# Routed experts of an FFT mixer: the last 20 tiles in steps of 64 tokens, second products on halves of the array

## The chip, the cores and the metric

The program runs on one core of a Trainium2 chip. The metric is the device time of the whole program in microseconds, median of three runs, lower is better. The profile is that of one more execution on the same core.

## What is computed

The input is `x` (8 sequences of 2496 tokens with 256 channels). Each sequence goes through a Fourier mixer, and every token of the result through one of eight experts:

```python
X = rfft(x, axis=1)
Yr = Xr @ w_r - Xi @ w_i + b_r          # likewise Yi
Yr = sign(Yr) * maximum(abs(Yr) - 0.01, 0)
y = irfft(Yr + 1j * Yi)                 # 19968 tokens of 256 channels
...
e_idx = argmax(y @ w_gate, axis=1)      # one expert of 8 for each token
for e in range(8):
    h = maximum(y[e_idx == e] @ w1[e], 0)      # 256 -> 1024: the first product
    ye = h @ w2[e]                             # 1024 -> 256: the second product
    out[e_idx == e] = gate_w * eom * ye
```

The products of the experts are made in float16 with a correction: each operand is split into a high and a low half, and three of the four partial products are added up (high x high, high x low, low x high).

## The kernel before

The kernel transforms the eight sequences one after the other. The routing sorts the tokens by expert and fills tiles of 128 tokens, each of one expert; this is done twice, once for the first four sequences (64 tiles, worked on in pairs that share an expert) and once for the rest (99 tiles, worked on singly), 163 tiles in all (`T_ALL`). The tiles of the first group fill gaps of the transform of the later sequences; from some 600 us on, the tail of the program is nearly all experts' tiles.

For each tile: `gathers` fetches 128 rows of `y` by an indirect DMA from GpSimd; `tokens` scales and splits them (VectorE, ScalarE), and a transposing DMA turns them, so that the channels lie on the partitions (`eT`); `fetch` loads the expert's weights into one of three buffers (`wbuf`), first half for `up`, second half for `down`.

`up` makes the first product. It is called twice for a single tile (`half`), each call filling one PSUM bank with 4 groups of 128 of the 1024 hidden channels. The stationary operand of each matmul is a block of 128x128 weights, the moving one is the tile's 128 tokens; a group is 6 matmuls (2 halves of the channels x 3 partial products), so a tile has 48. ScalarE then takes the bank to float16 with a Relu (L1489), VectorE writes what is lost by this rounding (L1490); the two are the high and low half of `hh`.

`down` makes the second product: stationary are 128 hidden channels by 128 tokens of `hh`, moving are 128x256 weights, and 24 matmuls (8 groups x 3) add up in one bank of 128 tokens by 256 channels. ScalarE scales it (L1461), and GpSimd scatters the rows to the output by an indirect DMA (L1464).

The order of all this is made by a planner in the program (`Issue`), which simulates the engines with the costs that each step names (`yield "P", r, 1.34, f`) and issues instructions in the order in which its model serves them. Steps with the smallest due time (`r`) go first. The planner knows none of the instructions' shapes; it knows the costs alone. In the tail its order on TensorE is: `up` of two tiles (four calls), then `down` of these two, and so on; the last tile stands alone.

Every matmul of these functions is preceded on TensorE by a load of its stationary operand (LDWEIGHTS), which the profile lists as PEld.

## Time and profile before

| | |
|---|---|
| time, median of 3 runs | 1435.92 us (1435.58 to 1435.95) |
| profiled execution | 1436.6 us, span 1434.8 us, mean granted clock 0.992 |
| TensorE busy | 1399.4 us, 98% of the span |
| weight loads busy | 1273.4 us, 89% |
| VectorE, ScalarE, GpSimd busy | 978.2, 738.6 and 636.3 us |
| first products of single tiles (L1479, 128 columns) | 4752 matmuls, 219 ns each from start to modelled end |
| second products (L1445) | 3912 matmuls, 273 ns each |

A matmul's length in the profile runs from its start to a modelled end, and several are in flight at once. So the time that one takes of TensorE isn't its length but the distance between starts: (length of an unbroken run - length of one) / (count - 1). Rows of weight loads (PEld) lie beside the matmuls, and an idle time of zero means that the engine was never without work between instructions. The forty slices of the page show busy tenths of each engine over the span; PEclk is the clock that TensorE was granted.

### The profile page before, as it was taken

The numbers are of one execution on the slowest core, as the hardware profiler recorded it, in microseconds if no ns is written. First come the engines' busy times: TensorE is split into PE (matmuls) and PEld (weight loads), VectorE is DVE, ScalarE is ACT, GpSimd is POOL, SyncE is SP. The second block draws the span as 40 slices with busy tenths as digits, with TensorE's granted clock in tenths as the row PEclk, the third lists the DMA queues.
The fourth block names the chain that finished last, engine by engine and source line by source line (L and its number), as shares of the span: only waits on it lengthen the run. The fifth ranks groups of instructions, "written<-read, shape, count | busy, mean of one in ns | idle before, by whom it ended". The sixth has DMA issues, their size and how long they took to land.

```text
span 1434.8 us, 42626 instructions
## 1 busy us (share of the span) xinstructions
PE 1399.4 (98%) x16436; PEld 1273.4 (89%) x16436; DVE 978.2 (68%) x2796; ACT 738.6 (51%) x1413; POOL 636.3 (44%) x729
## 2 busy tenths in 40 slices
PE   4999999999999998999999999999999999999998
PEld 4998887898888887888888888999999999999998
DVE  4887767788999896788888765554545545455452
ACT  4777676778687764433343344333334334333342
POOL 2274556266477563345455443333333343333411
PEclk8999999999999999999999999999999999999999
DMA  7779899998988789935372374533364233642342
GB/s 199 176 172 221 204 213 215 230 233 209 224 205 211 172 234 204 245 99 134 100 160 75 98 169 105 108 73 83 72 161 106 76 82 96 167 133 75 79 113 83
DMA packets 285652, 215.66 MB, mean 150 GB/s; under 512 B 240918, under 2 KB 249240, under 8 KB 281097
## 3 DMA queue, kind: packets, MB, share of 16 engines
q1 hardware_dynamic: 268887, 168.87, 49.6%
q0 software_dynamic: 15872, 42.83, 12.1%
q8 instruction: 129, 2.11, 0.6%
q10 hardware_dynamic: 690, 1.24, 0.3%
q14 instruction: 74, 0.61, 0.2%
HBM read 337.45 MB, written 58.91 MB: 276 GB/s over the span
## 4 chain that ended last, share of the span: by engine, by line
PE 46%; issue 29%; POOL 14%; DVE 6%; DMA 2%; ACT 1%; POOLq 0%; SPq 0%; ACTq 0%; DVEq 0%
PE ps L755 11%; PE ps L1479 9%; PE ps L1445 8%; POOL out L1464 7%; POOL yg L1348 7%; PE ps L647 5%; PE ps L851 3%; PE ps L785 3%; PE ps L725 3%; DMA x<-in_x 1%; PE ps L896 1%; PE ps L690 1%; PE ps L749 1%; PE ps L1277 1%; DVE z L771 1%
## 5 line engine op out<-in xcount | busy, mean ns | idle before, releaser
L1479 PE MATMUL ps<-eT,wbuf 128*128 128x128 f16 (+1 forms) x6288 | 458.9, 232 | 0.4 <-DMA wbuf<-wd 0.4
L1445 PE MATMUL ps<-wbuf,hh 128*128 128x256 f16 x3912 | 453.2, 273 | 0.0
L1479 PEld LDWEIGHTS <-wbuf 128*128 128x128 f16 x6288 | 418.9, 98 | 19.9 <-DMA wbuf<-wd 0.6
L1445 PEld LDWEIGHTS <-hh 128*128 128x128 f16 x3912 | 378.8, 98 | 44.2 <-issue 0.2
L1490 DVE SCALAR_TENSOR_TENSOR hh<-ps,hh 128x512 f16<-128x512 f32 x326 | 224.8, 690 | 267.6 <-ACT hh L1489 267.4
L1489 ACT ACTIVATE hh<-ps 128x512 f16<-128x512 f32 x326 | 194.6, 597 | 287.7 <-PE ps L1479 282.2
L1464 POOL DMA_INDIRECT out<-o,sidx x163 | 163.4, 1003 | 281.5 <-ACT o L1461 258.1
L1348 POOL DMA_INDIRECT yg<-yd,gidx x163 | 161.5, 991 | 247.1 <-DVE yhl L1374 211.5
L755 PE MATMUL ps<-whl,xt 128*128 128x256 f16 x1920 | 223.1, 273 | 0.7 <-ACT xt L740 0.7
L755 PEld LDWEIGHTS <-xt 128*128 128x128 f16 x1920 | 187.7, 98 | 32.1 <-ACT xt L740 1.1
L1461 ACT ACTIVATE o<-ps,facs 128x256 f32<-128x256 f32 x163 | 77.2, 473 | 229.5 <-PE ps L1445 149.0
L1374 DVE SCALAR_TENSOR_TENSOR yhl<-yg,ys,yhl 128x256 f16<-128x256 f32 x163 | 81.4, 506 | 62.4 <-ACT yhl L1373 62.3
L647 PEld LDWEIGHTS ps<-f1t,x 117*128 117x128 f32 (+1 forms) x704 | 87.1, 201 | 18.1 <-issue 15.8
L647 PE MATMUL ps<-f1t,x 117*128 117x120 f32 (+1 forms) x704 | 90.5, 285 | 0.2 <-ACT ste L802 0.2
L1373 ACT ACTIVATE yhl<-yg,ys 128x256 f16<-128x256 f32 x163 | 81.6, 501 | 13.9 <-DVE ys L420 5.9
L775 POOL TENSOR_TENSOR zhl<-z,zhl 128x512 f16<-128x512 f32 x54 | 62.8, 1162 | 49.8 <-ACT zhl L773 47.4
L1052 POOL TENSOR_TENSOR wsp<-wr,wsp 128x512 f16<-128x512 f32 x62 | 74.3, 1198 | 5.2
L785 PE MATMUL ps<-gt,zhl 128*128 128x128 f16 x960 | 65.5, 220 | 6.5 <-ACT zhl L773 3.7
L851 PE MATMUL ps<-bdt,f4t 120*117 120x512 f16 x264 | 71.0, 384 | 0.1
L656 ACT ACTIVATE at<-ps,sx 128x480 f16<-128x480 f32 (+1 forms) x88 | 55.7, 649 | 28.9 <-PE ps L647 26.3
L785 PEld LDWEIGHTS <-zhl 128*128 128x128 f16 x960 | 58.5, 98 | 13.4 <-ACT zhl L773 4.5
L770 ACT ACTIVATE zhl<-ps,sc 128x512 f32<-128x512 f32 x80 | 54.8, 685 | 25.6 <-PE ps L755 22.1
(195 smaller groups left out, 1651.0 us busy)
## 6 DMA issues: line engine op xcount, KB each, us to landing
wbuf<-wd SPq DMA_DIRECT2D x262, 1024.0 KB
yd<-yt SPq DMA_DIRECT2D x120, 158.4 KB
x<-in_x SPq DMA_DIRECT2D x114, 156.0 KB
wr<-in_moe_w SPq DMA_DIRECT2D x32, 512.0 KB
wd<-wsp SPq DMA_DIRECT2D x64, 256.0 KB
yg<-yd,gidx POOLq DMA_INDIRECT x163, 7.5
eT<-yhl SPq DMA_TRANSPOSE x163
out<-o,sidx POOLq DMA_INDIRECT x163, 2.4
```

The costliest lines, as they stand in the source:

```text
L647: T.matmul(pv[:, dh, :, m * j:m * j + m], xs[:k, j0 + j, 128 * dh:128 * dh + 128], fw, start=True, stop=True)
L755: T.matmul(yp[:, 256 * j:256 * j + 256], xt_[:, v, 2 * dh + j, 64 - 64 * u:192 - 64 * u], whl[:, dh, vw, 256 * u:256 * u + 256], start=Fal ...
L785: T.matmul(bv[:, j], zhl[:, vz, c:c + 128], gt[:, 2 * p + j, v], start=(n == 0), stop=(n == 2))
L851: T.matmul(pt[:P3], w, src[:, :, :, vb_], start=(n == 0), stop=(n == 2))
L1348: yield "G", r + 5.6 * t - 30, 1.0, lambda: G.indirect_dma_start(out=yg, out_offset=None, in_=src, in_offset=bass.IndirectOffsetOnAxis(ap= ...
L1373: yield "A", r - 10, 0.5, lambda: A.activation(yhl[:, 0], yg[:, :256], AF.Copy, scale=s)
L1374: yield "D", r - 10, 0.48, lambda: V.scalar_tensor_tensor(yhl[:, 1], yg[:, :256], s, yhl[:, 0], ALU.mult, ALU.subtract)
L1445: T.matmul(st["pt", t][1][:, :256], hh[:, v, fc, 128 * n:128 * n + 128], w[:, fc // 2, vw, fc % 2], start=(fc == k == 0), stop=(fc == 7 an ...
L1464: yield "G", r - DN, 1.0, lambda: G.indirect_dma_start(out=outs[t % 8], out_offset=bass.IndirectOffsetOnAxis(ap=sidx[:, t:t + 1], axis=0), ...
L1479: T.matmul(pt[:, 128 * m * j:128 * m * (j + 1)], w[:, dh, g // 4, vw, 128 * (g % 4):128 * (g % 4) + 128], eT[:, :m, v, dh], start=(n == 0) ...
L1489: yield "A", r, 0.6, lambda: A.activation(hv[:, 0], pt, AF.Relu)
L1490: yield "D", r, 0.69, lambda: V.scalar_tensor_tensor(hv[:, 1], pt, 0.0, hv[:, 0], ALU.max, ALU.subtract)
```

## The change

In the last 20 tiles (`t >= T_ALL - 20`), `up` writes each group of 128 columns in two steps of 64 tokens: all six matmuls for tokens 0 to 63, then all six for tokens 64 to 127. The weight blocks are loaded for each step anew, so a tile has 96 matmuls of 64 moving columns and 96 loads of 128x128 instead of 48 and 48.

`down` splits the stationary operand: for each of the 24 pieces there is one matmul for tokens 0 to 63, which writes PSUM partitions 0 to 63, and one for tokens 64 to 127, which writes partitions 64 to 127, both with the same 256 moving columns. The program marks the first as using columns 0 to 63 of the array and the second as using columns 64 to 127 (divisions of 128 rows by 64 columns), in turns. A tile has 48 matmuls and 48 loads of 64 columns instead of 24 and 24. All other matmuls of the program use the full array.

The costs that the planner is told stay the same, and so the order of steps on all engines does; the numbers of instructions on ScalarE, VectorE, GpSimd and SyncE are unchanged. On TensorE there are 34410 instructions where there were 31530 (20 tiles x 72 more matmuls and as many loads).

```diff
+HALVES = 20
 ...
 def down(t, m, n, w, hh, ih, r):
+        c = 64 if t >= T_ALL - HALVES else 128
         ...
             for fc in range(8 // m * half, 8 // m * (half + 1)):
                 for k, (v, vw) in enumerate(((0, 0), (0, 1), (1, 0))):
-                    T.matmul(st["pt", t][1][:, :256], hh[:, v, fc, 128 * n:128 * n + 128], w[:, fc // 2, vw, fc % 2], start=(fc == k == 0), stop=(fc == 7 and k == 2))
+                    for q in range(0, 128, c):
+                        T.matmul(st["pt", t][1][q:q + c, :256], hh[:, v, fc, 128 * n + q:128 * n + q + c], w[:, fc // 2, vw, fc % 2], start=(fc == k == 0), stop=(fc == 7 and k == 2))
 ...
 def up(t, m, half, w, eT, ie, hh, r):
-        c = 4 // m
+        cn = 4 // m
+        c = 64 if t >= T_ALL - HALVES else 128 * m
         def f(i):
             pt = bank(i)
-            for j in range(c):
-                g = c * half + j
-                n = 0
-                for dh in range(2):
-                    for vw, v in ((0, 0), (0, 1), (1, 0)):
-                        T.matmul(pt[:, 128 * m * j:128 * m * (j + 1)], w[:, dh, g // 4, vw, 128 * (g % 4):128 * (g % 4) + 128], eT[:, :m, v, dh], start=(n == 0), stop=(n == 5))
-                        n += 1
+            for j in range(cn):
+                g = cn * half + j
+                for q in range(0, 128 * m, c):
+                    n = 0
+                    for dh in range(2):
+                        for vw, v in ((0, 0), (0, 1), (1, 0)):
+                            tok = eT[:, :, v, dh] if m > 1 else eT[:, 0, v, dh, q:q + c]
+                            T.matmul(pt[:, 128 * m * j + q:128 * m * j + q + c], w[:, dh, g // 4, vw, 128 * (g % 4):128 * (g % 4) + 128], tok, start=(n == 0), stop=(n == 5))
+                            n += 1
             return pt
```

(In `up` the name `c` for the number of groups becomes `cn` in the lines behind it too.)

Two places in TensorE's order are shown. In the rows the line stands first, then the instruction; a matmul's row names the PSUM bank, the moving operand or weights and the shape as output partitions or rows by moving columns (128x64: 64 columns; 64x256: 64 output partitions). L1479 is L1486 after the change, L1445 is L1449. First, where `up` of two tiles ends and `down` begins (the first time both are changed), before:

```order
L1479 MATMUL ps1_25857<-eT0_9665,wbuf0_9304 128x128
L1479 LDWEIGHTS wbuf0_9304
L1479 MATMUL ps1_25857<-eT0_9665,wbuf0_9304 128x128
L1445 LDWEIGHTS hh1_9931
L1445 MATMUL ps4_25886<-wbuf2_9430,hh1_9931 128x256
```

and after:

```order
L1486 MATMUL ps1_26001<-eT0_9665,wbuf0_9304 128x64
L1486 LDWEIGHTS wbuf0_9304
L1486 MATMUL ps1_26001<-eT0_9665,wbuf0_9304 128x64
L1449 LDWEIGHTS hh1_9931
L1449 MATMUL ps4_26054<-wbuf2_9430,hh1_9931 64x256
```

Nothing moved past anything: the same steps follow each other, with the loads and matmuls of each made smaller and twice as many, and the division of the array changes with the line.

Second, where `down` of the two tiles ends and `up` of the next begins, before:

```order
L1445 MATMUL ps7_25688<-wbuf1_9305,hh0_9904 128x256
L1479 LDWEIGHTS wbuf2_9430
L1479 MATMUL ps3_25743<-eT0_9665,wbuf2_9430 128x128
L1479 LDWEIGHTS wbuf2_9430
L1479 MATMUL ps3_25743<-eT0_9665,wbuf2_9430 128x128
```

and after:

```order
L1449 MATMUL ps7_25736<-wbuf1_9305,hh0_9904 64x256
L1486 LDWEIGHTS wbuf2_9430
L1486 MATMUL ps3_25815<-eT0_9665,wbuf2_9430 128x64
L1486 LDWEIGHTS wbuf2_9430
L1486 MATMUL ps3_25815<-eT0_9665,wbuf2_9430 128x64
```

Here too the same steps follow each other; the first full-width load comes straight behind a matmul on the upper half of the columns. There are 11 stretches of changed second products between the first products, so 21 such places.

## The prediction

> **What bounds the kernel now.** I read the head of the page first: the share of each engine, and the forty slices with the granted clock.

> ```profile
> span 1434.8 us, 42626 instructions
> PE 1399.4 (98%) x16436; PEld 1273.4 (89%) x16436; DVE 978.2 (68%) x2796; ACT 738.6 (51%) x1413; POOL 636.3 (44%) x729
> ...
> PE   4999999999999998999999999999999999999998
> PEclk8999999999999999999999999999999999999999
> ```

> TensorE is busy in 98% of the span. The change touches only the end of it, so the next view is the windows of the last 135 us: span of the window, then busy time and count of PE, PEld, DVE, ACT and POOL, then clock, DMA share and GB/s.

> ```profile
> 1300.00:1350.00 50.00, 50.00 (x675) 47.36 (x673) 27.39 (x90) 19.56 (x38) 17.81 (x18) 1.00 0.33 74
> 1350.00:1400.00 50.00, 50.00 (x695) 47.57 (x693) 26.23 (x83) 19.76 (x38) 12.78 (x13) 1.00 0.39 105
> 1400.00:1435.00 35.00, 30.25 (x394) 28.06 (x392) 6.92 (x10) 9.29 (x17) 6.80 (x7) 0.97 0.27 85
> ```

> PE has no hole at all until its last matmul, at a clock of 1.00; VectorE is busy in about 53%, ScalarE in 39%, GpSimd in 26 to 36%, the DMA engines in 27 to 39%. So in this stretch the time is the sum of the starts of matmuls, and nothing else sets it. How far apart these starts lie is read from the timeline of PE (start, length, line, count of a run of like matmuls):

> ```profile
> 1309.80 3.85 PE L1479 MATMUL ps<-eT,wbuf 128*128 128x128 f16 x66
> 1313.49 5.40 PE L1445 MATMUL ps<-wbuf,hh 128*128 128x256 f16 x48
> 1318.73 5.52 PE L1479 MATMUL ps<-eT,wbuf 128*128 128x128 f16 x96
> 1324.09 5.40 PE L1445 MATMUL ps<-wbuf,hh 128*128 128x256 f16 x48
> ```

> and the groups of the stretch from 1230 us to the end, shapes apart (busy us, mean ns of one, idle before):

> ```profile
> L1445 PE MATMUL ps<-wbuf,hh 128*128 128x256 f16 x926 | 104.4, 273 | 0.0
> L1479 PE MATMUL ps<-eT,wbuf 128*128 128x128 f16 x1776 | 102.3, 219 | 0.0
> L1479 PEld LDWEIGHTS <-wbuf 128*128 128x128 f16 x1776 | 100.7, 98 | 0.4
> L1445 PEld LDWEIGHTS <-hh 128*128 128x128 f16 x923 | 89.4, 98 | 10.2
> L1490 DVE SCALAR_TENSOR_TENSOR hh<-ps,hh 128x512 f16<-128x512 f32 x75 | 51.7, 690 | 77.5 <-ACT hh L1489 77.5
> L1489 ACT ACTIVATE hh<-ps 128x512 f16<-128x512 f32 x74 | 44.2, 597 | 51.1 <-PE ps L1479 48.8 <-DVE hh L1490 2.2
> ```

> A single matmul lasts 219 or 273 ns, but they overlap. 96 first products take 5.52 us, so the spacing is (5.52 - 0.219)/95 = 55.8 ns; 48 second products take 5.40 us, so (5.40 - 0.273)/47 = 109.1 ns. Two tiles are 96 x 55.8 + 48 x 109.1 = 10.59 us, which is what the two starts of L1445 say (1324.09 - 1313.49 = 10.60). Each matmul has a weight load of 98 ns of its own, and none of these loads is seen in the spacing: the two spacings differ by 53.3 ns for 128 columns, 0.417 ns a column, and leave 2.4 ns a matmul. The run of second products also starts 56 ns after the last first product (1309.80 + 3.85 - 0.219 = 1313.43): going from one kind to the other costs nothing today.

> **The change, part by part.** Twenty tiles are 20 x 5.30 = 106 us, from about 1324 us to the last matmul. Their order, their waits, and every instruction of the other engines stay; only PE's stream changes.

> First products. Per two tiles 96 matmuls of 128 columns become 192 of 64, each with its own full load: the loads are doubled. By the two spacings a matmul of 64 columns takes 64 x 0.417 + 2.4 = 29.1 ns, if a load of 128 columns can be had in that time. The logits of the gate show that it can (L896, matmuls of 16 and 32 columns, each with a 128x128 load), and one other line has just 64 columns (L1277):

> ```profile
> 100.89 1.76 PE L896 MATMUL ps<-wg,bt 128*128 128x32 f16 x64
> 100.78 1.76 PEld L896 LDWEIGHTS <-bt 128*128 128x128 f16 x64
> L896 PE MATMUL ps<-wg,bt 128*128 128x32 f16 x352 | 20.4, 177 | 0.0
> 371.30 0.29 PE L1277 MATMUL ps<-ob,ol 117*128 117x64 f16 x4 [0.35 <-POOL ob L1269]
> 391.78 0.30 PE L1277 MATMUL ps<-ob,ol 117*128 117x64 f16 x4
> L1277 PE MATMUL ps<-ob,ol 117*128 117x64 f16 x88 | 6.8, 196 | 1.1 <-DVE ob L1269 0.7 <-POOL ob L1269 0.3
> ```

> 64 loads and matmuls in 1.76 us are (1.76 - 0.177)/63 = 25.1 ns a pair: the loads alone don't bound at 29. L1277 runs at (0.29 - 0.196)/3 to (0.30 - 0.196)/3, 31 to 35 ns, but its weights are columns of a strided array over 117 rows; those of L1479 lie side by side like L896's. I take 29.1: 192 x 29.1 = 5.59 for 5.36 us, +0.23 us per two tiles, **+2.3 us** in ten such pairs. The upper bound is 35 ns: 192 x 35 = 6.72, +13.6 us. The lower one is bare streaming, 26.7 ns, -2.3 us; the constant of 2.4 ns stands in both spacings, so I don't believe in it.

> Second products. 48 matmuls with 128 stationary columns become 96 with 64, by turns on the lower and upper half of the array's columns, each with its own load and again 256 moving columns. A column of time is now used by one half of the array only, unless two run at once. At once: a pair takes 109.1 ns, and the term is **0**. One after the other: a pair takes 218 ns, +109.1 x 24 x 20 = +52.4 us. The trace has no matmul on a part of the columns, so these are the ends, and a gain below 0 is excluded except for one constant of 2.4 ns per pair (-1.2 us), since either half still streams 256 columns. I take 0. Two matmuls are in flight on this engine already (273 ns long, 109 ns apart), so a start doesn't wait for an end; what spaces them is the streaming into one set of columns, and the two now have different ones and different PSUM partitions. The load is the smaller doubt: the only group of non-128 columns shows

> ```profile
> L851 PEld LDWEIGHTS <-f4t 120*117 120x117 f16 x264 | 31.5, 135 | 10.6 <-issue 0.9 <-DVE ste L803 0.2
> L851 PE MATMUL ps<-bdt,f4t 120*117 120x512 f16 x264 | 71.0, 384 | 0.1
> ```

> 135 ns for 117 columns where 128 take 98: such loads are slower, but two of 64 columns have the whole 109 ns of a pair as cover.

> [...]

> Switches between the two divisions of the array. In this order of work (four runs of first products, two of second ones) there are 21 changes from full width to halves or back. Bounds: 0, as between L1479 and L1445 today; or PE runs empty and the load that was hidden lies bare: into the first products 273 - 109 + 98 = 262 ns, into the second ones 196 - 29 + up to 135 = 302 ns, on the mean 0.28 us, 21 x 0.28 = 5.9 us. I take 0.25 us, **+5.3 us**: the overlap in the low row is that of loads and matmuls of one geometry, and with another geometry the load has no free place to go to while full-width matmuls are in the array. [...]

> Nothing follows PE that becomes late in a new way. The end hangs on its last matmul as before:

> ```profile
> 1427.41 2.84 PE L1445 MATMUL ps<-wbuf,hh 128*128 128x256 f16 x24
> 1430.29 0.47 ACT L1461 ACTIVATE o<-ps,facs 128x256 f32<-128x256 f32 x1 [2.08 <-PE ps L1445]
> 1431.04 0.97 POOL L1464 DMA_INDIRECT out<-o,sidx  x1 [4.34 <-ACT o L1461]
> ```

> and the activations, splits and weight fetches behind and ahead of PE only get more room.

> The sum: +2.3 + 0 + 5.3 = +7.6 us. The profiled execution took 1436.6 us (span 1434.8), 0.7 above the median of 1435.92 that it is compared with; on the median I get **1443.5 us**, +0.5%. About 0.2% (2.9 us) is what a measurement of this kernel can tell from no change.

> **The rivals.**
> 1. The halves run one after the other, since matmuls start in order and stream through one input. For it: no row shows two streams. Then +52.4 with the first products' 2.3, and 0 to 5.9 for switches: 1491 to 1497 us.
> 2. Halves run at once, but the load for a half can't go into it while its own matmul streams, and lies bare between them. Against it: at full width 98 ns of load are hidden within 56 ns spacings. For it: a divided array is not shown to have that room. A pair takes 109 + 98 = 207 ns: 24 x 20 x 98 = +47 us, with the rest 1485 to 1491 us. [...]
> 3. On the other side: not slower. Switching halves costs nothing, as between the two lines today, and only the 2.3 us are left: 1438 us. The point that decides is (2.9 - 2.3)/21 = 28 ns a switch; below that the change can't be told from none.

> **How the numbers follow.** The forecast (halves at once, switches dear, 1438.8 to 1450) 0.46; rival 3 (1437 to 1438.8) 0.2; rival 1 0.15; rival 2 0.13; a partial overlap, 1450 to 1485, 0.06. The forecast and rival 3 hold only 0.66, so the range must reach over rival 2: 1437 to 1491 us leaves out most of rival 1. The likeliest case's own range is 1438.8 to 1450. Faster by over 0.2% needs a gain that no row offers: 0.02. Within: rival 3, 0.2. Slower: 0.78.

> **What would show it.** First products: runs of 192 with a spacing of 29 ns and no idle PEld. Second products: 96 matmuls of 64x256 in 5.2 to 5.5 us, pairs of starts close together; if they start evenly 109 ns apart, rival 1 holds; with loads between them and pairs 207 apart, rival 2. Switches: a gap of some 0.25 us in starts at each change of line, or 56 ns as today. I am wrong at once if the loads for half the columns aren't hidden, or if 384 short instructions in a row can't be fed (L896 shows 128 in 1.76 us, no more).

## The result and the profile after

The changed kernel takes 1443.1 us in the median (1442.1 to 1443.94), against 1435.75 us for the kernel before measured beside it: a ratio of 1.0052, 95% interval 1.0035 to 1.0070, slower by about 7.4 us. The profiled execution took 1443.94 us. The head of its page:

```profile
span 1442.2 us, 45507 instructions
PE 1404.2 (97%) x17876; PEld 1281.2 (89%) x17876; DVE 977.8 (68%) x2796; ACT 738.4 (51%) x1413; POOL 636.8 (44%) x729
```

TensorE is busy 4.8 us longer, but the span has grown by 7.4: 2.6 us more of it are idle. The timeline of PE through the changed tiles shows where both come from (start, length, line, operands, count, and the idle time before):

```profile
1313.80 5.40 PE L1449 MATMUL ps<-wbuf,hh 128*128 128x256 f16 x48
...
1329.98 5.77 PE L1486 MATMUL ps<-eT,wbuf 128*128 128x64 f16 x192
1335.68 5.43 PE L1449 MATMUL ps<-wbuf,hh 128*64 128x256 f16 x96
1341.04 5.77 PE L1486 MATMUL ps<-eT,wbuf 128*128 128x64 f16 x192
...
1385.31 4.87 PE L1486 MATMUL ps<-eT,wbuf 128*128 128x64 f16 x161
1392.32 1.06 PE L1486 MATMUL ps<-eT,wbuf 128*128 128x64 f16 x31 [2.14 <-issue]
1393.31 5.43 PE L1449 MATMUL ps<-wbuf,hh 128*64 128x256 f16 x96
```

Two tiles take 1341.04 - 1329.98 = 11.06 us where they took 10.60. Taken apart:

- First products: (5.77 - 0.193)/191 = 29.2 ns a matmul; 1920 x 29.2 - 960 x 55.8 = +2.5 us.
- Second products: 96 matmuls last 5.43 us where 48 lasted 5.40. The single starts in the trace lie 3 to 4 and 105 to 106 ns apart by turns: the two halves run at once, and a pair takes 109 ns, as a full-width matmul did. Only the second pair of each stretch starts 24 ns late (130 ns in place of 106). On the mean that makes (5.43 - 0.273 - 0.004)/47 = 109.6 ns a pair; 480 pairs, +0.25 us, all of it next to a change of division.
- Changes of division: from the last first product to the first second one 123 ns (29 within the first products), from the last second one to the next first one 205 ns (109 a pair), the same at all 20 of these changes to within 1 ns. That is 94 and 96 ns more. The first of the 21 changes lies inside second products, since of its two tiles only one is changed; it takes 202 ns in place of 109. Together +2.0 us. The records of the loads show what is held up: in runs of full-width matmuls a load starts 1 to 2 ns behind the matmul ahead of it, but the first load of a new division starts 122 ns (into the second products) and 201 ns (out of them) behind the last matmul's start. The first matmul starts 1 to 5 ns after that.
- One hole inside a run of first products, after 161 of 192: 1392.32 - (1385.31 + 4.87 - 0.193) = 2.33 us between two starts, with no wait that the trace could name ("issue"). +2.3 us.

The sum is 7.05 us. From the start of the last unchanged pair's second products (1313.80 us; 1313.49 before) to that of the very last ones (1434.78; 1427.41 before) it is 120.98 us where it was 113.92, +7.06; the other 0.3 us of the span's difference lie ahead of the changed tiles. The groups of the changed stretch, and who waited (second fence: us in total, times, longest):

```profile
L1486 PE MATMUL ps<-eT,wbuf 128*128 128x64 f16 x1848 | 56.0, 193 | 2.1 <-issue 2.1
L1449 PE MATMUL ps<-wbuf,hh 128*64 128x256 f16 x960 | 54.5, 273 | 0.0
L1449 PEld LDWEIGHTS <-hh 128*64 128x64 f16 x960 | 51.5, 110 | 0.8 <-issue 0.2
```

```profile
PE ps L1486 <- issue: 2.1, 1, 2.1
PEld L1486 <- issue: 4.2, 11, 2.2
```

A load of 64 columns lasts 110 ns where one of 128 lasts 98, and none of it shows. The loads of the first products were held up eleven times, once for 2.2 us (the hole) and ten times for 0.2 us: the changes from halves to full width.

The hole comes in the middle of a heavy transfer, the new expert's weights. Windows of 4 us around it (PE, PEld, DVE, ACT, POOL, clock, DMA share, GB/s):

```profile
1378.00:1382.00 4.00, 4.00 (x108) 3.95 (x105) 3.56 (x13) 1.59 (x3) 0.00 (x0) 1.00 0.11 25
1382.00:1386.00 4.00, 4.00 (x86) 3.80 (x83) 0.68 (x2) 1.34 (x3) 0.97 (x1) 1.00 0.40 78
1386.00:1390.00 4.00, 4.00 (x144) 4.00 (x141) 2.25 (x8) 1.41 (x3) 0.97 (x1) 1.00 1.03 309
1390.00:1394.00 4.00, 1.86 (x52) 1.72 (x50) 1.53 (x4) 1.30 (x3) 0.00 (x0) 1.00 1.02 289
```

The same page counts the DMA packets that bring instructions on queue 8, 16 KB each (before: 129, 2.11 MB); 11 came to them with the 2880 instructions that came to TensorE:

```profile
q8 instruction: 140, 2.29, 0.7%
```

Among the DMA records of the trace these packets start 3.6 to 7.3 us apart in the changed stretch, but the one ahead of the hole starts at 1389.76 us, 9.1 us after the last; TensorE goes on 2.56 us later. A late packet alone doesn't make a hole: in the kernel before the packet at 1388.39 us comes 13.0 us after the last, during the same loads, and TensorE doesn't stop. There two tiles use 288 instructions in 10.60 us, here 576 in 11.06. The theory that was tested is the author's estimate from these counts, since no record shows how many instructions TensorE holds ready: at twice as many instructions per microsecond it runs out of them when a packet comes late, and the packet comes late while an expert's weights are loaded.

### The profile page after: what moved, and what is told of

Read it like the earlier page. It is cut to its first block, busy times and chain, and to the rows that moved or that the text cites. A ratio compares the mean times of both kernels' runs of the same rounds, so it can differ in the third digit from the quotient of the medians.

```text
span 1442.2 us, 45507 instructions
## 1 busy us (share of the span) xinstructions
PE 1404.2 (97%) x17876; PEld 1281.2 (89%) x17876; DVE 977.8 (68%) x2796; ACT 738.4 (51%) x1413; POOL 636.8 (44%) x729
## 5 line engine op out<-in xcount | busy, mean ns | idle before, releaser
L1486 PE MATMUL ps<-eT,wbuf 128*128 128x128 f16 (+2 forms) x7248 | 461.5, 223 | 2.5 <-issue 2.1
L1449 PE MATMUL ps<-wbuf,hh 128*128 128x256 f16 (+1 forms) x4392 | 453.5, 273 | 0.0
L1486 PEld LDWEIGHTS <-wbuf 128*128 128x128 f16 x7248 | 421.1, 98 | 23.8 <-issue 4.2
L1449 PEld LDWEIGHTS <-hh 128*128 128x128 f16 (+1 forms) x4392 | 384.0, 100 | 39.5 <-issue 0.4
L648 PEld LDWEIGHTS ps<-f1t,x 117*128 117x128 f32 (+1 forms) x704 | 87.1, 201 | 15.9 <-issue 13.6
L771 ACT ACTIVATE zhl<-ps,sc 128x512 f32<-128x512 f32 x80 | 54.8, 685 | 25.1 <-PE ps L756 21.7
```

What stands on the lines that cost most here:

```text
L648: T.matmul(pv[:, dh, :, m * j:m * j + m], xs[:k, j0 + j, 128 * dh:128 * dh + 128], fw, start=True, stop=True)
L1449: T.matmul(st["pt", t][1][q:q + c, :256], hh[:, v, fc, 128 * n + q:128 * n + q + c], w[:, fc // 2, vw, fc % 2], start=(fc == k == 0), stop ...
L1486: T.matmul(pt[:, 128 * m * j + q:128 * m * j + q + c], w[:, dh, g // 4, vw, 128 * (g % 4):128 * (g % 4) + 128], tok, start=(n == 0), stop= ...
```

## The experiments

Each is the changed kernel with the edit shown, unless another is named. Ratios are to the kernel before on the same chip. Chips differ: the first four kernels under "Without the weight loads" ran on one where the kernel before takes 1448.5 us, all others on one where it takes 1436 to 1437 us.

**Only the first products** (`u20`).

```diff
 def down(...):
-        c = 64 if t >= T_ALL - HALVES else 128
+        c = 128
```

> Only the first products of the last 20 tiles go by 64 columns; the second ones stay at full width. Theory: the 64-column matmuls start every 29.2 ns as in the changed kernel, 1920 x 29.2 - 960 x 55.8 = +2.5 us, there is no extra gap where the lines change (56 ns as before), and in executions in which TensorE's instructions come late during the weight loads near 1385 us another 2 us: 1438.3 or 1440.5 us. Rival: the gap of about 0.1 us at each change of line comes from the short matmuls and not from the division of the array; then the gaps stay, +4.5 us, 1440.3 us without a late fetch.

Measured: 1440.3 us (1438.15 to 1447.89), 1.0043 (1.0026 to 1.0060). The timeline of PE:

```profile
1326.69 5.76 PE L1486 MATMUL ps<-eT,wbuf 128*128 128x64 f16 x192
1332.29 5.41 PE L1449 MATMUL ps<-wbuf,hh 128*128 128x256 f16 x48
1337.53 5.76 PE L1486 MATMUL ps<-eT,wbuf 128*128 128x64 f16 x192
...
1387.85 0.83 PE L1486 MATMUL ps<-eT,wbuf 128*128 128x64 f16 x23 [1.88 <-issue]
1388.52 7.07 PE L1449 MATMUL ps<-wbuf,hh 128*128 128x256 f16 x48
```

Two tiles take 10.84 us, +0.24. There is no gap at the changes of line (29 and 109 ns between starts, as within a run), so the gap doesn't come from short matmuls. A hole is there again, and this time the second products behind it take 7.07 us in place of 5.41: the trace's clock records have the granted clock at half for 3.41 us from 1388.84 us on. So the hole costs 2.0 us here and 1.7 more by the clock. That makes some 1442 us; the slowest run, 1447.9 us, isn't explained by one such hole.

**Only the second products** (`d20`).

```diff
 def up(...):
-        c = 64 if t >= T_ALL - HALVES else 128 * m
+        c = 128 * m
```

> Only the second products of the last 20 tiles go by halves in turns; the first ones stay at 128 columns. Theory: pairs of 109.7 ns (+0.3 us in 480 pairs) and 21 changes of division at 0.094 us more each (+2.0 us), TensorE takes instructions a quarter slower in the first products than in the changed kernel, so no late fetch: 1438.1 us. Rival, the prediction's price: 0.25 us a change, 1441.3 us. Rival, gaps come from the short matmuls: 1436.1 us.

Measured: 1438.25 us, 1.0019 (1.0009 to 1.0028), +2.2 us between medians.

```profile
1329.91 5.53 PE L1486 MATMUL ps<-eT,wbuf 128*128 128x128 f16 x96
1335.37 5.43 PE L1449 MATMUL ps<-wbuf,hh 128*64 128x256 f16 x96
1340.74 4.47 PE L1486 MATMUL ps<-eT,wbuf 128*128 128x128 f16 x77
```

Two tiles take 10.83 us, +0.23. Between starts there are 149 ns into the second products (56 before: +93) and 205 out of them (109: +96). No hole. The price of a change is thus the same with long and with short matmuls, 0.095 us, and the prediction's 0.25 falls.

**Both products by halves** (`g20`): the first products too use the halves of the columns in turns, so that nothing changes between the lines.

```diff
 def up(...):
-                for q in range(0, 128 * m, c):
-                    ...
+                for dh in range(2):
+                    for vw, v in ((0, 0), (0, 1), (1, 0)):
+                        for q in range(0, 128, 64):
+                            T.matmul(pt[q:q + 64, 128 * j:128 * (j + 1)], w[:, dh, g // 4, vw, 128 * (g % 4) + q:128 * (g % 4) + q + 64], eT[:, 0, v, dh], ...)
```

> Both products of the last 20 tiles are made by halves of the array's columns in turns (the first ones with 64 of the 128 hidden channels stationary and all 128 tokens moving), so the division stays the same over all 20 tiles and changes once. Theory: the gaps of 0.094 us at the changes of line are gone (-2.0 us against the kernel with only the second products divided); if a pair of 64-column loads fits into 55.8 ns, the time is 1436.2 us. If a load of 64 columns holds the load path for 27 ns each, 54 ns a pair fit just so; if for 53 ns, a pair takes 107 ns and the first products double: 960 x 51 ns = +49 us, 1485 us. Rival, the gap belongs to the change from one line to the other and not to the division: the gaps stay.

Measured: 1438.84 us (1436.86 to 1443.37), 1.0020 (1.0011 to 1.0028).

```profile
1333.50 5.53 PE L1485 MATMUL ps<-eT,wbuf 128*64 128x128 f16 x192
1338.86 5.41 PE L1449 MATMUL ps<-wbuf,hh 128*64 128x256 f16 x96
1344.10 1.12 PE L1485 MATMUL ps<-eT,wbuf 128*64 128x128 f16 x34
...
1386.50 4.69 PE L1485 MATMUL ps<-eT,wbuf 128*64 128x128 f16 x161
1393.55 1.05 PE L1485 MATMUL ps<-eT,wbuf 128*64 128x128 f16 x31 [2.36 <-issue]
```

Two tiles take 1344.10 - 1333.50 = 10.60 us, just what they took undivided, and the gaps between the lines are gone (the division changes three times in the first pair, where one tile is still undivided, and then no more). So working in halves costs TensorE nothing as long as the division stays; two loads of 64 columns fit into 55.8 ns. The time is still 2.6 us above the 1436.2 us that were expected. In this execution the changed tiles lose 2.58 us between two starts in the hole; it is the slowest of the twelve, and another 3.8 us of it lie ahead of the changed tiles (the first pair begins at 1322.55 us, before at 1318.73). That the hole makes up the median's difference too is likely, but not shown.

**Second products in halves, but not in turns** (`d20_seq`), and in **runs of 8 and 12** (`d20_run8`, `d20_run12`), each from the kernel with only the second products divided:

```diff
 def down(...):                      # d20_seq
-            for fc in ...:
-                for k, (v, vw) in ...:
-                    for q in range(0, 128, c):
+            for q in range(0, 128, c):
+                for fc in ...:
+                    for k, (v, vw) in ...:
                         T.matmul(...)
 def down(...):                      # d20_run8; 12 in the other
+            piece = [...]           # the 24 pieces in their order
+            for b in range(0, len(piece), 8):
+                for q in range(0, 128, c):
+                    for fc, k, v, vw in piece[b:b + 8]:
                         T.matmul(...)
```

> As the kernel with only the second products divided, but not in turns: all 24 matmuls of a tile on the lower half of the columns first, then the 24 on the upper. Same instructions, same number of changes. Theory: two matmuls run at once only because neighbours in the order lie on different halves; now each waits for the one ahead on its half, 109 ns each: 20 x 24 x 109.1 = +52.4 us more than in turns, about 1490 us. Rival: the engine finds work for the idle half further back in its queue, or the load of one half is what is shared; then it stays near 1438 us, or lies between.

Measured: 1479.1 us, 1.0306 (1.0291 to 1.0321), +43 us. That lies between the theory's 1490 and the 1438 us of no loss: four fifths of the loss that was expected against turns (40.9 of 52.4 us), and the missing fifth is regular. In the timeline a stretch of two tiles

```profile
1335.39 9.45 PE L1449 MATMUL ps<-wbuf,hh 128*64 128x256 f16 x96
```

takes 9.45 - 0.273 = 9.18 us between its first and last start, where 96 in a row at 109 ns would take 10.4. In the single starts there are three places, one for each change of half, where over four matmuls of 109 ns twice as many start; if the order of the program were kept strictly, only the two neighbours at the border would overlap. The author's estimate from this is four places for each half, and it was tried with shorter runs.

> Second products alone by halves, in runs of 8: eight matmuls on the lower half, eight on the upper, and so on. Theory after the run with 24 and 24: each half has a queue of its own of 4 matmuls (one at work, three behind it), filled in program order; a run of R on one half then lets the other start when 4 are left, a pair takes max(R, 2(R - 4))/R x 109 ns. With R = 8 no loss but an offset of 4 x 109 ns at the end of each of 11 stretches: 2.3 + 4.8 = +7.1 us. Rival, in order without such queues, so that only the two matmuls at a border overlap: (2 x 8 - 1)/8 x 109 = 205 ns a pair, +46 us.

> The same in runs of 12. Theory of 4 places a half: runs start 872 ns apart, so a stretch of two tiles takes 7 x 0.872 + 12 x 0.109 = 7.41 us in place of 5.23; over 20 tiles +21.8 us, with the 2.3 of the division +24 us. Rival of places without limit: as with 8. Rival of none: (2 x 12 - 1)/12 x 109 = 209 ns a pair, +48 us.

Measured: with runs of 8 1447.66 us, 1.0085 (1.0064 to 1.0106), +10.8 us; with runs of 12 1462.2 us, 1.0178 (1.0158 to 1.0198), +25.3 us. The stretches of two tiles, first with 8, then with 12:

```profile
1332.63 6.20 PE L1450 MATMUL ps<-wbuf,hh 128*64 128x256 f16 x96
1338.76 5.53 PE L1487 MATMUL ps<-eT,wbuf 128*128 128x128 f16 x96
```

```profile
1335.16 7.82 PE L1450 MATMUL ps<-wbuf,hh 128*64 128x256 f16 x96
1342.91 5.53 PE L1487 MATMUL ps<-eT,wbuf 128*128 128x128 f16 x96
```

With 12, 7.82 - 0.273 = 7.55 us between the first and last start; with none to look ahead it would be some 10. With 8, 5.93 us: most of the loss that strict order would bring (+46 us) isn't there. The figures expected from the estimate (7.41 for 12) count one spacing too many for this distance. From first to last start four places a half give 9.05 us for runs of 24, 7.31 for 12 and 5.56 for 8; measured are 9.18, 7.55 and 5.93. In the single starts each change of half costs 30 ns on top, and the second matmul of the stretch starts 24 ns late, both of which the estimate lacked. With 3, 7 and 11 changes of half that makes 9.17, 7.54 and 5.92 us. The records don't say which half a matmul is on, so the four places are worked out from the time that is saved, not seen.

**Without the weight loads.** The changed kernel and, as a control, the kernel before lose the loads of their last 24 tiles, and the kernel with both products by halves is stretched to 96 tiles, with the loads and without.

```diff
 def fetch(r):
-                    nc.sync.dma_start(W[wplace(k)][:, part], ...)
+                    if t < T_ALL - HALVES - 4:      # g96_noload: without the 4
+                        nc.sync.dma_start(W[wplace(k)][:, part], ...)
```

> The changed kernel, but the weight loads (wbuf from wd) of the last 24 tiles are left out, so these tiles compute with whatever expert's weights lie in the buffers. Theory: the hole of 2.2 us in TensorE's stream at 1390 us comes from a late fetch of its own instructions, which queues behind the 1 MB weight loads of an expert change; without these loads no hole in any execution, and only 2.5 us (64 columns), 0.3 (pairs) and 2.0 (changes of division) are left: +4.8 us, 1440.8 us, with little scatter. Rival: the hole belongs to a place in the instruction stream (161 matmuls into a run of first products), whatever the DMA queues do; then it stays, about 1443 us.

> The control: the kernel before, with the weight loads of the last 24 tiles left out in the same way. Theory: TensorE has no hole there before, so nothing changes: 1436 us. Rival: the loads cost the kernel before something too (SBUF or HBM traffic beside the matmuls); then it is faster by what the kernel without loads gains for that reason alone.

> Both products by halves of the columns in turns, for the last 96 tiles in place of 20. Theory: the division and the pairs cost nothing (0 us in five times as many tiles, two tiles still take 10.60 us); late fetches come at the expert changes, about seven of them in 96 tiles, each 2 to 3 us and 1 to 1.5 more where the clock falls behind the hole: +10 to +25 us, 1446 to 1461 us. Rival: the holes come by chance or by place and not at expert changes; then about 5 in places that have no weight load. Second rival: the pairs do cost a little (0.1 us in a tile would be 10 us, evenly spread).

> As the kernel with 96 tiles by halves, with the weight loads of these tiles left out. Theory: no holes, 1436 us, equal to the kernel before although TensorE issues twice as many instructions for 500 us. Rival: the holes stay.

Measured, beside 1448.51 us for the kernel before on this chip: the changed kernel without the loads 1458.92 us, 1.0071 (1.0052 to 1.0091), +10.4 us where +4.8 was expected; the control 1451.07 us, 1.0012 (0.9999 to 1.0025); 96 tiles by halves 1492.49 us, 1.0290 (1.0271 to 1.0310), without loads 1487.49 us, 1.0257 (1.0238 to 1.0275). The times here say little on the theory: this chip has holes of another sort, 0.3 to 0.8 us between starts, in the control too. PE's waits with no named cause (total, times, longest) of the control, of the 96 tiles with loads, and of those without:

```profile
PE ps L1480 <- issue: 4.5, 15, 0.5
```

```profile
PE ps L1485 <- issue: 23.2, 62, 1.1
PE ps L1449 <- issue: 3.2, 2, 2.0
```

```profile
PE ps L1486 <- issue: 17.1, 46, 0.5
```

In the 96 tiles they come about once in two tiles, whether weights are loaded or not; their cause wasn't looked for. Those over 0.33 us cost some 27 us in the kernel without loads, but some 8 us in the control as well, so they explain about half of its 39 us, and the rest is open. So the expected +10 to +25 us of 96 tiles and the 0 us without loads are both missed on this chip. Long holes are another matter: with loads there are five (1.17 to 2.23 us between starts, each ended 2.4 to 2.8 us after the start of an instruction packet), without loads none over 0.75 us, neither in the 96 tiles nor in the changed kernel, and the two kernels of 96 tiles differ by 5.0 us. For two of the five (1.17 and 1.30 us) the packet came 5.8 and 6.2 us after the last, no later than others, so a late packet isn't seen at each.

**The same pair again, on a chip without those short holes** (`a20_again`: no edit; `a20_noload2`: as above; the kernel before takes 1436.87 us).

> The changed kernel once more, beside the one without weight loads on the same chip, since chips differ by some 12 us. Theory: +4.8 us (columns, pairs, changes of division) in executions without a late fetch of instructions, 1.2 to 3.5 us more where TensorE waits for one; the profile shows such a hole over 1 us during the weight loads of an expert change, ended 2.4 to 2.8 us after the start of a 16 KB instruction packet. Rival: no such hole here; then the hole of the first profile was chance.

> The changed kernel without the weight loads of its last 24 tiles (they compute with what lies in the buffers), on the same chip as the changed kernel. Theory: no hole over 1 us, and 1 to 3 us less than the changed kernel. Rival: equal times and the hole stays.

Measured: the changed kernel 1444.07 us, 1.0053 (1.0037 to 1.0070); without loads 1441.25 us, 1.0033 (1.0022 to 1.0044): +7.2 and +4.4 us. The intervals overlap, so the verdict rests on the profiles. The changed kernel:

```profile
1382.48 4.87 PE L1486 MATMUL ps<-eT,wbuf 128*128 128x64 f16 x161
1389.29 1.76 PE L1486 MATMUL ps<-eT,wbuf 128*128 128x64 f16 x31 [1.93 <-issue]
1390.98 6.29 PE L1449 MATMUL ps<-wbuf,hh 128*64 128x256 f16 x96
```

```profile
1385.00:1389.00 4.00, 2.35 (x81) 2.26 (x78) 3.56 (x11) 1.59 (x3) 0.00 (x0) 1.00 1.05 340
1389.00:1393.00 4.00, 3.71 (x53) 3.33 (x54) 1.12 (x6) 0.60 (x1) 0.00 (x0) 0.57 0.56 117
```

and the same place without the loads:

```profile
1384.44 5.77 PE L1487 MATMUL ps<-eT,wbuf 128*128 128x64 f16 x192
1390.14 5.43 PE L1450 MATMUL ps<-wbuf,hh 128*64 128x256 f16 x96
```

```profile
1387.00:1391.00 4.00, 4.00 (x127) 3.95 (x125) 3.56 (x12) 2.19 (x4) 0.00 (x0) 1.00 0.07 24
```

With the loads (340 GB/s) the run of 192 breaks after 161, for 2.12 us between starts, ended 2.33 us after an instruction packet that itself started 9.4 us after the last one; behind it the clock is at 0.57 on the mean of 4 us. Without them the run is whole, at the same place in the program. The hole doesn't belong to the place, but to the place and the transfer together. From the second products ahead of the changed tiles to the last ones it is 122.34 us with the loads (1310.97 to 1433.31) and 118.68 without (1312.93 to 1431.61): 8.42 and 4.76 us more than the 113.92 of the kernel before, where +4.8 was expected without a hole. The first profile of the change, `u20` and `g20`, in which the first products have twice as many instructions too, have such a hole in the same run of first products, after 161 or 169 of 192 matmuls. So it is four profiles with the loads against one without.

## Why the prediction was right, and where it wasn't

The total was forecast at 1443.5 us and came at 1443.1, with the forecast's case (halves at once) and the sign as given. Two terms of the sum were wrong and cancelled each other: 5.3 us were forecast for the changes of division and 2.0 found, 0 for a late supply and 2.3 found. That the total came within half a microsecond is luck.

- The bound (TensorE's starts alone): right. In the profile without a hole (`a20_noload2`) nothing but the starts makes up the time, and the parts found alone, +0.24 (`u20`) and +0.23 us (`d20`) per two tiles, give the +0.46 of both.
- First products, +2.3 us at 29.1 ns: right, 29.2 ns and +2.5 us.
- Second products, 0: right. The +0.25 us are the late second pair of each stretch. Rivals 1 and 2 are out: the starts come in pairs 4 ns apart and 109 ns a pair, with the loads hidden. `d20_seq` shows what most of rival 1 would have cost: +43 us.
- Changes of division, +5.3 us: mis-sized. They are real and belong to the division (none between the lines in `u20` and `g20`, the same in `d20`), but cost 0.095 us each, +2.0 us. (With the late starts just behind the changes it is 0.11 us each: from the second products ahead of the changed tiles to the last ones `d20` takes 116.28 us, the kernel before 113.92.) No run shows the 0.25 us a change that the sum uses, nor the reason given for it, a load without a free place; what the runs show in its place is 93 to 96 ns more between starts. The step that failed is "PE runs empty and the load that was hidden lies bare". The load does start late, 122 or 201 ns behind the last matmul in place of 1 to 2, but its 98 to 110 ns aren't added, since the first matmul starts 1 to 5 ns after it, and PE isn't seen to run empty: 205 ns from start to start are less than the 273 that the profile gives one matmul, so the next division begins before the modelled end of the last matmul.
- Nothing behind or ahead of PE that is late: wrong. The instruction supply was named only among the things that would prove the text wrong, with no price in the sum. The hole that is put down to it cost 2.3 us in the profiled execution and, with the clock behind the hole, more in others (2.0 and 1.7 us in `u20`). The run of L896 (128 instructions in 1.76 us) was too short to show it: in `g96` 54 more packets came with 13824 more instructions, 256 to each. The rate alone isn't the trouble, since without the loads the same rate leaves no hole.
- Rival 3 (not slower): its condition was under 28 ns a change; at 95 ns it fell. `g20`, which takes all but three of the changes away, is the nearest to it: two of its tiles take 10.60 us, as before.

What the packet does is in part argued. In these runs the long hole comes only with the weight loads, and each one ends 2.3 to 2.8 us after the start of an instruction packet; in the four profiles with 20 changed tiles that packet starts 9.0 to 10.4 us after the last. That it waits behind those of the weights at the DMA engines would fit, but it isn't shown: the records don't name the engine of a packet.

## What to carry to other kernels

Here two matmuls of half the stationary columns took what one full one did, with neighbours in the program's order on the two halves of the array (109 ns a pair within a stretch, 109.1 ns a full one). Keep the turns short, since runs of 8, 12 and 24 on one half took 10.8, 25.3 and 43 us more than the kernel before where turns of one took 2.2, and the division constant, since each change cost 0.095 us. Price the short matmul by the slope and constant of two longer ones, and see that the load keeps up in a run with still shorter ones. When a change doubles instructions on a saturated engine, count its instruction packets as well as its columns (11 more here, with a hole of 2.3 us behind a late one), and look where large transfers fall.
